# Pooled attention and a gated convolution FFN on one core: first k as words over SyncE, w_in whole over GpSimd, first expansion tiles split at 128 tokens, and a new written order

## The chip, the core and the metric

The kernel runs on one core of one Trainium2 chip. The core has TensorE (PE; its weight loads are shown apart as PEld), VectorE (DVE), ScalarE (ACT), GpSimd (POOL) and SyncE (SP), and 16 DMA engines, which loads and stores share. The metric is the device time of one execution in microseconds (us).

## What is computed

Eight batches, each of 8 heads, 576 tokens and 64 channels per head. k and v are averaged over groups of 8 tokens (72 groups), q attends to the averages, and the result, 576 x 512 per batch, goes through a gated FFN with a depthwise convolution of three taps along the tokens:

```python
k_p = k.reshape(B, H, Sp, pool, D).mean(axis=3)
v_p = v.reshape(B, H, Sp, pool, D).mean(axis=3)
attn = softmax(q @ k_p^T / sqrt(D))
x = attn @ v_p                          # heads side by side: (B, S, 512)
h = np.maximum(x @ w_in, 0.0)           # 512 -> 1024
conv_out[s] = sum(conv_w[t] * h[s + t - 1] for t in (0, 1, 2))
out = (h * sigmoid(conv_out)) @ w_out   # 1024 -> 512
```

Inputs and output are fp32; the kernel computes in bf16 with fp32 sums.

## The kernel before, in words

Everything is one list of small operations, each added to a `Planner` with its engine, what it reads and what it writes. Their order is not found at build time: `PARAMS["order"]` is a long string of operation numbers, written out, and the operations are issued in that order, so each engine runs its own share of the list strictly one after the other. An entry such as `17A1/159@B1` means: 17 fills (matmuls of zeros into PSUM buffer A1, line 227), then operation 159, whose result goes to PSUM buffer B1. There are five PSUM buffers, A0 to A2 (two banks) and B0, B1 (one bank); an operation that takes a buffer waits until the last reader of its former content is done. `PARAMS["act"]` lists the operations that could run on either engine and run on ACT; the others run on DVE. `PARAMS["alt"]` picks one of several ways for some steps.

Per batch b the steps are:

- Loads. k (`load_k`, lines 265 and 269), v (`load_v`, 277 and 282) and q (`load_q`, 246 and 251) go over POOL, which converts fp32 to bf16 on the way. Batches use the buffers `k_b`, `v_b`, `q_b` in turns of two. POOL's loads carry one of eight semaphores in turn, so each load waits until the one eight places ahead of it has landed.
- k: `pool8` adds eight tokens in steps on DVE (414, 418, 443, the sum `ksum`), PE transposes it (459), and two copies put it into `kz` (465). v: the same on DVE (414, 418, 491; for batch 0, 479 and 483), then two multiplications by a mask into `vblk` (503, 508). There is a second way, `by_identity`, in which PE adds the eight tokens by eight matmuls with the identity and one copy follows.
- q: PE transposes (525 for batch 0, 545 for others), copies bring it to `qT` (531, 552).
- Scores (583, 585; 602, 604), exponentials on ACT (591, 610), product with v on PE (628, 632), division by the sum on DVE (641 the reciprocal, 645 the multiplication into `xx`), transposition on PE (659) with a copy (663), or from batch 3 on by a transposing DMA on SP (668).
- Expansion `mm1` (685 for batch 0, 700 for others) with ReLU on ACT (691, 706). For batch 0 a block of 128 hidden units is done in two groups of tokens, 0 to 383 and 384 to 575, so that the first can start before the last tokens are there.
- Convolution, either by multiplications and additions (`conv_off`, 722 to 741) or on PE with diagonal matrices `dw` (`conv_pe`, 753; the matrices are made at 384 and 386), gate on ACT (741, 758), multiplications on DVE (785, 791).
- Output `mm2` (813), copy (836, 826), store on SP (840, 831) from one of three buffers `osb`.

At the start, the first two of four slices of the first half of w_in come as fp32 words over SP (line 290) and are converted by two copies (294); the other two come over POOL (301), the second half of w_in too (306).

## Time and profile before

| | |
|---|---|
| three runs | 198.35, 198.59, 198.66 us (median 198.59) |
| profiled execution | 199.99 us, span from first to last instruction 198.3 us |
| busy in the span | PE 190.1, DVE 164.1, ACT 172.0, POOL 48.3 us |
| granted TensorE clock, mean | 1.00 |
| read from device memory, written | 32.5 MB, 9.4 MB |

The page lists engines' busy time, the chain of work that ended last, and groups of instructions by line. The timeline lists instructions in order of time: start, length, engine, line, operation, result<-operands with shape and type, how many were merged, and in brackets how long the engine stood idle before and what ended that. Lengths of neighbours on one engine can overlap by 0.1 us or so, since they are pipelined.

### The profile page before, as it was taken

The page shows a single profiled execution, that of the slowest core. Times are in us where ns is not written, and L with a number is a line of the kernel's source. Part 1 is how long each engine was busy: PE and PEld are TensorE (multiplying, and loading weights), DVE is VectorE, ACT ScalarE, POOL GpSimd, SP SyncE. Part 2 cuts the span into 40 slices and gives each one's busy share as a digit, 9 for nine tenths or more (in the row PEclk, how much of TensorE's full clock was granted, in tenths as well). Part 3 has the DMA queues.
Part 4 walks back from the last instruction along what each step waited for, and adds up shares of the span by engine and source line. Part 5 has one row for each costly group of instructions (what it writes and reads, how often), then busy time and mean ns, then how long its engine had stood idle before and what let it go on. Part 6 is the DMA issues. An engine that isn't in the chain of part 4 may idle for free.

```text
span 198.3 us, 4826 instructions
## 1 busy us (share of the span) xinstructions
PE 190.1 (96%) x1890; PEld 132.3 (67%) x1905; DVE 164.1 (83%) x375; ACT 172.0 (87%) x314; POOL 48.3 (24%) x87
## 2 busy tenths in 40 slices
PE   7899989999999999999999999999999999999992
PEld 7897866776677878856866665766666655555441
DVE  3246759999949999999899999999999999899620
ACT  0559999992679999999999999999999899999931
POOL 7878425347225630080006100000000000000000
PEclk9999999999999999999999999999999999999999
DMA  6999999999999999999987999691401844043244
GB/s 134 169 135 150 188 205 205 206 191 142 204 196 185 152 192 60 197 113 197 172 232 158 194 213 166 120 164 26 172 3 27 266 144 161 1 148 117 106 164 159
DMA packets 40763, 30.41 MB, mean 153 GB/s; under 512 B 18572, under 2 KB 36004, under 8 KB 40740
## 3 DMA queue, kind: packets, MB, share of 16 engines
q0 software_dynamic: 18272, 16.00, 56.5%
q1 hardware_dynamic: 22468, 14.11, 31.4%
q8 instruction: 15, 0.25, 0.5%
q14 instruction: 8, 0.07, 0.1%
HBM read 32.52 MB, written 9.44 MB: 212 GB/s over the span
## 4 chain that ended last, share of the span: by engine, by line
PE 48%; ACT 16%; DMA 14%; DVE 12%; POOL 4%; issue 4%; ACTq 0%; DVEq 0%; POOLq 0%
PE psfA L700 16%; PE psfB L813 14%; DMA k_b<-in_k_dram 10%; ACT tg L741 5%; DMA v_b<-in_v_dram 4%; PE psfA L628 4%; ACT cv L722 3%; ACT hT L706 3%; PE psfA L753 2%; PE psfA L602 2%; ACT osb L836 2%; DVE cv L724 2%; POOL v_b L282 2%; DVE gT L791 2%; PE psfA L632 2%
## 5 line engine op out<-in xcount | busy, mean ns | idle before, releaser
L813 PE MATMUL psfB<-w_out,gT 128*128 128x512 bf16 (+1 forms) x259 | 62.6, 377 | 1.0 <-issue 0.2
L700 PE MATMUL psfA<-xT,w_in 128*128 128x288 bf16 x448 | 61.9, 286 | 0.1
L700 PEld LDWEIGHTS <-w_in 128*128 128x128 bf16 x448 | 43.0, 98 | 13.1 <-issue 0.8
L813 PEld LDWEIGHTS <-gT 128*128 128x128 bf16 x290 | 27.7, 98 | 28.8 <-DVE gT L791 1.0
L741 ACT ACTIVATE tg<-cv,cs 128x576 bf16<-128x576 bf16 x54 | 41.2, 789 | 0.3
L706 ACT ACTIVATE hT<-psfA 128x576 bf16<-128x576 f32 x56 | 36.6, 665 | 1.4 <-PE psfA L700 0.9
L645 DVE TENSOR_TENSOR xx<-psfA,rr 128x512 bf16<-128x512 f32 x40 | 27.1, 686 | 0.7
L722 ACT ACTIVATE cv<-hT,cr 128x576 bf16<-128x576 bf16 x35 | 26.9, 783 | 0.1
L724 DVE TENSOR_SCALAR cv<-hT,cr 128x576 bf16<-128x576 bf16 x73 | 25.9, 377 | 0.9 <-ACT hT L706 0.7
L282 POOL DMA_DIRECT2D v_b<-in_v_dram x32 | 16.8, 531 | 33.9 <-DVE vs L491 31.1
L836 ACT COPY osb<-psfB 128x512 f32<-128x512 f32 x33 | 19.2, 591 | 5.9 <-PE psfB L813 5.5
L791 DVE TENSOR_TENSOR gT<-tg,hT 128x1152 bf16<-128x1152 bf16 x32 | 23.9, 751 | 0.3
L610 ACT ACTIVATE attnT<-psfA 128x576 bf16<-128x576 f32 x35 | 22.7, 675 | 0.3
L734 DVE TENSOR_TENSOR cv<-cv 128x1152 bf16<-128x1152 bf16 (+1 forms) x29 | 20.7, 713 | 1.0 <-ACT cv L722 0.3
L729 DVE TENSOR_TENSOR cv<-cv,hT 128x1152 bf16<-128x1152 bf16 (+1 forms) x29 | 20.6, 711 | 0.3 <-ACT cv L722 0.2
L227 PEld LDWEIGHTS <-zero 128*128 128x128 bf16 x238 | 15.6, 105 | 1.7 <-DVE zero L318 1.1
L628 PE MATMUL psfA<-vblk,attnT 128*128 128x130 bf16 x160 | 15.9, 221 | 0.4 <-DVE xx L645 0.3
L785 DVE TENSOR_SCALAR tg<-tg 128x1152 bf16<-128x1152 bf16 x32 | 14.2, 448 | 2.2 <-ACT tg L741 2.0
L628 PEld LDWEIGHTS <-attnT 128*128 128x128 bf16 x160 | 11.8, 98 | 4.4 <-DVE xx L645 0.6
L227 PE MATMUL pswA<-zero 128*128 128x128 bf16 x192 | 13.3, 235 | 1.1 <-DVE zero L318 1.1
L414 DVE TENSOR_TENSOR k_b<-k_b 128x1280 bf16<-128x1280 bf16 x8 | 6.7, 840 | 6.8 <-DMA k_b<-in_k_dram 6.8
L641 DVE RECIPROCAL rr<-psfA 128x8 f32<-128x8 f32 x40 | 7.7, 198 | 5.2 <-PE psfA L632 5.1
(95 smaller groups left out, 234.1 us busy)
## 6 DMA issues: line engine op xcount, KB each, us to landing
out_dram<-osb SPq DMA_DIRECT2D x14, 512.0 KB, 3.2
k_b<-in_k_dram POOLq DMA_DIRECT2D x8, 512.0 KB, 8.5
q_b<-in_q_dram POOLq DMA_DIRECT2D x7, 576.0 KB, 8.2
v_b<-in_v_dram POOLq DMA_DIRECT2D x7, 512.0 KB, 12.2
out_dram<-osb SPq DMA_DIRECT2D x7, 256.0 KB, 2.1
w_out<-in_moe_w_out_dram POOLq DMA_DIRECT2D x2, 512.0 KB, 11.8
wf<-in_moe_w_in_dram SPq DMA_DIRECT2D x1, 512.0 KB, 5.3
k_b<-in_k_dram POOLq DMA_DIRECT2D x8, 64.0 KB, 6.3
```

The costliest lines, as they stand in the source:

```text
L227: nc.tensor.matmul(out=t, lhsT=zero[:, 0:P], rhs=zero[:, 0:P], start=True, stop=True)
L610: nc.scalar.activation(out=at(m)[:, t, :].rearrange("p (r i j) -> p r i j", i=2, j=3), in_=slot(key)[:, :, 0:HC].rearrange("p i (j r) -> p ...
L628: nc.tensor.matmul(out=a[:, g, c * w:(c + 2) * w], lhsT=attnT[m][:, S * s + u0:S * s + u0 + P], rhs=vblk[m][:, 2 * s:2 * s + 2, :].rearran ...
L645: nc.vector.tensor_tensor(out=xx[i3].rearrange("p (g h e) -> p g h e", g=2, h=4), in0=av_view()[:, :, :, 0:D], in1=rr[i3].rearrange("p (g ...
L700: nc.tensor.matmul(out=t[:, i, 0:HC], lhsT=w_in[:, c, f * P:(f + 1) * P], rhs=xT[m][:, c, i * HC:(i + 1) * HC], start=(c == 0), stop=(c == ...
L706: nc.scalar.activation(out=hT[m][:, f, 2:S + 2].rearrange("p (i x) -> p i x", i=2), in_=slot(key)[:, :, 0:HC], func=ACT.Relu)
L722: nc.scalar.activation(out=cv[y][:, kk // 2, z, :], in_=src, func=ACT.Copy, scale=sc)
L724: nc.vector.tensor_scalar(out=cv[y][:, kk // 2, z, :], in0=src, scalar1=sc, scalar2=None, op0=OP.mult)
L741: nc.scalar.activation(out=tg[i3][:, z, :], in_=cv[y][:, 0, z, :], func=ACT.Tanh if half else ACT.Sigmoid, scale=cs[:, f + z:f + z + 1] if ...
L791: nc.vector.tensor_tensor(out=o_, in0=tg[i3], in1=hT[b % 2][:, f:f + 2, 2:S + 2], op=OP.mult)
L813: nc.tensor.matmul(out=a[:, 0, j0:j1], lhsT=g[:, c, t * P:(t + 1) * P], rhs=w_out[:, c, j0:j1], start=(c == 0), stop=(c == n_fb - 1), skip ...
L836: copy_on(e)(out=osb[i3][:, x, :], in_=slot(key)[:, 0, :])
```

## The change

- k of batch 0 comes as fp32 words over SP (three loads, ahead of nearly everything) into the three output buffers `osb`, which are free until the first output. DVE's first addition reads the words there and writes bf16 into `k_b` (three instructions, one per buffer), and goes on as before.
- The first half of w_in comes whole over POOL with conversion; the words over SP and the two copies go.
- In the expansion of batch 0 the group of tokens 0 to 383 of the first four blocks of hidden units is split at 128 tokens, so that its first part needs only the first 128 tokens.
- v of batch 1 is summed on PE (`alt`: `"v1": 1`).
- `order` and `act` are written anew over the whole program; fills go from 238 to 167.

```diff
 "order": (
-    "59 0 45 58 2 40 49 46 39 50 41 57 56 48 13 1 16 3 57A0/4@B0 17 5 43 18 6 12A0/83@B0 36 53 7 20 52 84 55 61 69 38 23 54 28 14 73 25 "
+    "50 0 49 59 2 45 52 46 60 51 47 54 53 74 48 72 55 57 58 13 73 16 75 1 76 56 3 99A0/77@B0 39 14 78 15 79 20A0/80@B1 17 86 82@B0 40 "
...
-"alt": {"w": 1, "q1": 1, "c0.5": 2,
+"alt": {"q1": 1, "v1": 1, "c0.5": 2,
...
-    wf = st("wf", [P, n_dc, 512], FP32)
+    wf = st("wf", [P, 2, 512], FP32)
...
     def load_k(b):
-        m = b % 2
+        m = b % NK
         src = rows(k, b)
+        if b == 0:
+            for x in range(2):
+                def fn(e, x=x):
+                    nc.sync.dma_start(out=osb[x], in_=src[256 * x:256 * x + 256].rearrange("(t p) e -> p t e", p=P))
+                pl.add(f"ldkf{x}", "SP", 0.5, fn, writes=[("osb", x, 0), ("osb", x, 1)], dma=(256, 0.104, 16))
+
+            def fn(e):
+                nc.sync.dma_start(out=osb[2][0:64, 0, :], in_=src[512:576])
+            pl.add("ldkf2", "SP", 0.5, fn, writes=[("osb", 2, 0)], dma=(64, 0.104, 16))
+            return
...
+        def whole():
+            def fn(e):
+                nc.gpsimd.dma_start(out=w_in[:, :, 0:512], in_=src[:, :, 0:512])
+            pl.add("ldwi", "POOL", 0.8, fn, writes=[("wi", 0, c) for c in range(n_dc)], dma=(512, 0.087, 16))
...
         def on_dve():
-            pool8(b, "k", src, keys)
+            if b == 0:
+                for x, n in enumerate((2, 2, 1)):
+                    def fn(e, x=x, n=n):
+                        nc.vector.tensor_tensor(out=src[:, 2 * x:2 * x + n, 0:256], in0=osb[x][:, 0:n, 0:256], in1=osb[x][:, 0:n, 256:512], op=OP.add)
...
-                for c in range(n_dc):
-                    nc.tensor.matmul(out=t[:, 0, 0:n], lhsT=w_in[:, c, f * P:(f + 1) * P], rhs=xT[m][:, c, j0:j1],
+                wk = [("wi", f // 4, c) for c in range(n_dc)]
+                cut = P if x == 0 and f < 4 else 0
+                for a0, a1, ts_ in ((0, cut, ts[0:1]), (cut, n, ts[1 if cut else 0:])):
...
+                        for c in range(n_dc):
+                            nc.tensor.matmul(out=t[:, 0, a0:a1], lhsT=w_in[:, c, f * P:(f + 1) * P], rhs=xT[m][:, c, j0 + a0:j0 + a1],
```

In the pieces below a row is an instruction of one engine in its order: number, line, operation, result<-operands, shape, and the semaphores that it waits for; `_75` and `_76` are the two `v_b`, `_73` and `_74` the two `k_b`, `_77` and `_78` the two `q_b`.

POOL's first loads before, right behind the constants, and what stands ahead of q of batch 1 and w_in further on:

```order
6 L246 DMA q_b_77<-in_q_dram 32x8x384
7 L265 DMA k_b_73<-in_k_dram 128x4x512
8 L269 DMA k_b_73<-in_k_dram 64x512
9 L246 DMA q_b_77<-in_q_dram 64x8x384
10 L282 DMA v_b_75<-in_v_dram 16x512 [waits DVE_49]
...
29 L277 DMA v_b_75<-in_v_dram 128x2x512 [waits DMASW2_49]
30 L375 AFFINE_SELECT mask<-mask 128x4x65
31 L251 DMA q_b_78<-in_q_dram 96x8x384 [waits DMASW3_49]
32 L269 DMA k_b_74<-in_k_dram 64x512 [waits DMASW4_49]
33 L301 DMA w_in<-in_moe_w_in_dram 128x2x512 [waits DMASW5_49]
34 L265 DMA k_b_74<-in_k_dram 128x4x512 [waits DMASW6_49]
```

And now:

```order
6 L248 DMA q_b_77<-in_q_dram 64x8x384
7 L248 DMA q_b_77<-in_q_dram 32x8x384
8 L289 DMA v_b_75<-in_v_dram 128x2x512 x2
9 L294 DMA v_b_75<-in_v_dram 16x512 [waits DVE_49]
...
18 L389 AFFINE_SELECT mask<-mask 128x260
19 L253 DMA q_b_78<-in_q_dram 96x8x384 [waits DMASW0_49]
...
26 L302 DMA w_in<-in_moe_w_in_dram 128x4x512 [waits DMASW1_49]
27 L281 DMA k_b_74<-in_k_dram 64x512 [waits DMASW2_49]
28 L277 DMA k_b_74<-in_k_dram 128x4x512 [waits DMASW3_49]
```

k of batch 0 is gone from POOL, so q and v of batch 0 stand first, and q of batch 1, w_in and k of batch 1 stand behind loads that were issued at the very start.

The start of ACT before:

```order
1 L384 ACT_TABLE_LOAD [waits DVE_49]
2 L384 ACTIVATE dw_113<-ident,cw 128x128 [waits Pool_49]
3 L384 ACTIVATE dw_119<-ident,cw 128x128
4 L531 COPY qT_86<-psbB 128x24x32 [waits PE_49]
5 L294 COPY w_in<-wf 128x512 [waits DMAHW0_49]
```

The start of ACT now (L498 is the copy into `kz`, L564 that into `qT`, L624 the exponentials):

```order
1 L498 ACT_TABLE_LOAD [waits DVE_49]
2 L498 COPY kz_84<-psbB 64x4x72 [waits PE_49]
3 L498 COPY kz_84<-psbB 64x4x72
4 L564 COPY qT_86<-psbB 128x12x64 [waits PE_49] x2
5 L564 COPY qT_86<-psbA 128x24x32 [waits PE_49]
6 L624 ACTIVATE attnT_88<-psfB 128x384 [waits PE_49]
7 L624 ACTIVATE attnT_88<-psfA 128x384 [waits PE_49]
```

The `dw` matrices and the casts of w_in no longer come first; the table load stands with the copies of `kz`, and both halves of `kz` and all of `qT` are on ACT.

DVE between v of batch 4 and v of batch 6 now (L524 ends the sum of v, L434 and L438 are its first two additions):

```order
163 L524 TENSOR_TENSOR vs<-v_b_75 128x320
...
186 L772 TENSOR_TENSOR cv_102<-cv_102 128x1152
187 L434 TENSOR_TENSOR v_b_75<-v_b_75 128x5x256
...
191 L434 TENSOR_TENSOR v_b_76<-v_b_76 128x5x256
...
195 L438 TENSOR_TENSOR v_b_76<-v_b_76 128x5x128
...
213 L438 TENSOR_TENSOR v_b_75<-v_b_75 128x5x128
```

Before, with the lines of that kernel (L491, L414, L418):

```order
154 L491 TENSOR_TENSOR vs<-v_b_75 128x320
...
166 L414 TENSOR_TENSOR v_b_76<-v_b_76 128x5x256
...
178 L418 TENSOR_TENSOR v_b_76<-v_b_76 128x5x128
...
180 L414 TENSOR_TENSOR v_b_75<-v_b_75 128x5x256
```

v of batch 6 (`v_b_75`) is added ahead of v of batch 5 (`v_b_76`) instead of behind it, 24 rows behind the sum that frees its buffer instead of 26.

On PE the entry ahead of the transposes of k of batch 1 is `17A1/159@B1` where it had no fill, and the next expansion has 12 more.

81 lines of the change are left out of this document (49 added, 32 removed), and 93 rows, old and new, of the table PARAMS.

## The prediction

> **What bounds the kernel now.** I read the stretches first, then the order of time in the first 30 us, then the chain and the DMA issues. The stretches give busy time in the order PE, PEld, DVE, ACT, POOL, then the granted clock, the DMA share and GB/s.
>
> ```profile
> 0.00:24.00 24.00, 21.84 (x414) 19.84 (x414) 12.04 (x38) 14.30 (x36) 18.21 (x39) 1.00 0.98 154
> 30.00:45.00 15.00, 14.73 (x189) 10.98 (x187) 14.58 (x32) 14.39 (x30) 6.60 (x13) 1.00 1.23 199
> 45.00:190.00 145.00, 143.58 (x1223) 95.49 (x1235) 134.80 (x297) 134.77 (x229) 21.99 (x35) 1.00 0.84 146
> ```
>
> From 45 to 190 us PE is busy for 143.6 of 145.0 us, and DVE and ACT for 134.8 each: PE sets the pace there. From 30 to 45 us all three are full. In the first 24 us PE looks busy too, but most of that is fill (matmuls of zeros). So the time is the moment at which real PE work starts, plus the PE work behind it. What holds that start back is data:
>
> ```profile
> 2.08 8.71 DMA k_b<-in_k_dram
> 11.26 1.00 DVE L414 TENSOR_TENSOR k_b<-k_b 128x1280 bf16<-128x1280 bf16 x1 [3.62 <-DMA k_b<-in_k_dram]
> 13.25 0.49 DVE L443 TENSOR_TENSOR ksum<-k_b 128x640 bf16<-128x640 bf16 x1
> 14.32 0.45 PE L459 MATMUL psbA<-ident,ksum 128*128 128x128 bf16 x5
> 16.41 0.87 ACT L591 ACTIVATE attnT<-psfB 128x384 bf16<-128x384 f32 x2
> 19.05 0.40 PE L628 MATMUL psfA<-vblk,attnT 128*128 128x130 bf16 x4
> 23.99 0.82 PE L685 MATMUL psfB<-xT,w_in 128*128 128x384 bf16 x4
> ```
>
> The first row is of the chain that ended last, the others of the timeline (start, length). k of batch 0 is issued at 2.08 and lands at 10.79; DVE has waited 3.62 us for it; the sum over eight tokens is done at 13.74, the first exponential starts at 16.41, the first product with v at 19.05, the first expansion (L685) at 23.99. A second wait for data follows at k of batch 1:
>
> ```profile
> 16.03 11.00 DMA k_b<-in_k_dram
> 27.12 0.83 DVE L414 TENSOR_TENSOR k_b<-k_b 128x1280 bf16<-128x1280 bf16 x1 [3.17 <-DMA k_b<-in_k_dram]
> 28.30 0.49 PE L685 MATMUL psfA<-xT,w_in 128*128 128x192 bf16 x4
> 29.28 0.45 PE L459 MATMUL psbA<-ident,ksum 128*128 128x128 bf16 x5 [0.50 <-DVE ksum L443]
> ```
>
> **The change, step by step.** *k of batch 0.* It becomes 1.18 MB of words on SP's queue in place of a conversion on POOL's. The nearest rows are the words of w_in, which go, and the stretches in which they moved:
>
> ```profile
> 0.81 0.45 SPq L290 DMA_DIRECT2D wf<-in_moe_w_in_dram  x1
> wf<-in_moe_w_in_dram SPq DMA_DIRECT2D x1, 512.0 KB, 5.3
> 1.37 0.72 POOL L246 DMA_DIRECT2D q_b<-in_q_dram  x1 [0.86 <-POOLq L905]
> 3.00:4.00 1.00, 1.00 (x12) 1.00 (x11) 0.00 (x0) 0.00 (x0) 1.00 (x2) 1.00 0.88 302
> 4.00:5.00 1.00, 1.00 (x17) 1.00 (x15) 0.00 (x0) 0.00 (x0) 1.00 (x6) 1.00 1.30 220
> ```
>
> Issued at 0.81, 512 KB land 5.3 us later, at 6.1. Their bytes are through by about 4.8, so some 1.2 us of this is tail. The other 0.66 MB of k follow on the same queue: at the 302 GB/s of the fourth microsecond they take 2.2 us and land at 8.2; at half of the 220 GB/s of the fifth, which q then shares, 6.0 us and land at 12.0. I take 8.6, near the undisturbed end, because q, issued at 1.37, left the words nearly all of the fourth microsecond. The rule that speaks against this is in the Trainium skill (DMA: Bandwidth & Descriptors, Queues, rings and completion order): each DMA engine takes the queues that have work in turns, packet by packet. By that rule the half-share end is the likelier one and the sum would be that of the third rival below; the fifth microsecond, where the total fell to 220 GB/s with both queues at work, agrees as far as it goes.
>
> DVE then adds 128x512 elements from fp32 (L463, the last of three; the other two wait for earlier landings), halves again and sums. Prices from rows of the same size:
>
> ```profile
> 19.85 0.69 DVE L645 TENSOR_TENSOR xx<-psfA,rr 128x512 bf16<-128x512 f32 x1
> 12.78 0.44 DVE L418 TENSOR_TENSOR k_b<-k_b 128x640 bf16<-128x640 bf16 x1
> ```
>
> 8.6 + 0.69 + 0.44 + 0.49 = 10.2 for the sum, against 13.74: 3.5 us earlier.
>
> *ACT's first instruction.* Before, ACT loaded its function table while nothing waited. In the new order the load stands ahead of the copies of kz and waits with them for DVE's memset of kz (the order on ACT shows both), which is behind the sum and identf:
>
> ```profile
> 7.13 1.28 ACT L384 ACT_TABLE_LOAD   x1 [7.13 <-DVE cw L338]
> 6.16 0.38 DVE L330 CAST identf<-ident 24x24 f32<-24x24 bf16 x1 [3.55 <-POOL ident masks.py:199]
> 2.04 0.30 DVE L391 MEMSET kz<- 128x288 uint32 x1
> 15.57 0.39 ACT L465 COPY kz<-psbA 64x288 bf16<-64x288 bf16 x1
> 14.05 1.50 ACT L531 COPY qT<-psbB 128x768 bf16<-128x768 bf16 x2 [2.25 <-PE psbB L525]
> ```
>
> 10.2 + 0.38 + 0.30 = 10.9, + 1.28 = 12.2, two kz copies 0.78, three qT copies 3 x 0.75: the first exponential starts at 15.2, against 16.41. Of 3.5 us, 1.2 are left, since copies that stood beside other work are now in a row. The casts of w_in leave ACT (0.62 and 0.69 us); here nothing waits for them.
>
> *Exponentials to first expansion.* Before, 16.41 to 19.05 is 2.6 us. In the new order two scores reuse PSUM buffers that an exponential frees, and one more exponential and one dw stand ahead: about 3.1, so the first product with v starts at 18.3. From there the first expansion follows after five normalisations, whose last frees its PSUM buffer: two products (0.5 + 0.4), then five times 0.69, five reciprocals and a dw of 0.2 each, less some 0.5 of overlap: about 5.1 us, against 4.94. It starts at 23.4, **0.6 us earlier**. Splitting a 384-token group at 128 costs four weight loads more per block; by the L628 row above, four 130-column matmuls take 0.40 with their tail, so 0.1 each, 0.4 for four blocks. w_in, now whole over POOL, is no stop: its two neighbours ahead are out earlier, because POOL is no longer held by k.
>
> ```profile
> 13.98 0.80 POOL L251 DMA_DIRECT2D q_b<-in_q_dram  x1
> 15.31 0.75 POOL L301 DMA_DIRECT2D w_in<-in_moe_w_in_dram  x1
> 13.00:14.00 1.00, 0.76 (x36) 0.63 (x36) 0.71 (x2) 0.00 (x0) 0.99 (x3) 1.00 0.39 37
> ```
>
> Eight loads of 0.5 to 0.8 us and POOL's masks end at about 10, so q of batch 1 is issued near 10 where it was 13.98, w_in near 11.5 (15.31), k of batch 1 near 13 (16.03). The hole at 13 us (37 GB/s) closes, and k of batch 1 lands some 3 us earlier; the wait of 0.50 us ahead of L459 goes. If it doesn't, these 0.5 us stay.
>
> *Fill.* The four blocks end at 28.4 (28.79 before). But the new order puts 17 fills ahead of the transposes of k of batch 1; 23 took 1.33 us, so 17 take 1.0:
>
> ```profile
> 14.56 1.33 PEld L227 LDWEIGHTS <-zero 128*128 128x128 bf16 x23
> ```
>
> L459 starts at 29.4, 0.1 later than before. So the whole gain of the start is spent here, unless these fills stand in a wait anyway.
>
> *From there to the first output product.* The rows of before:
>
> ```profile
> 39.51 0.81 DVE L414 TENSOR_TENSOR v_b<-v_b 128x1280 bf16<-128x1280 bf16 x1
> 40.36 0.49 DVE L418 TENSOR_TENSOR v_b<-v_b 128x640 bf16<-128x640 bf16 x1
> 40.89 0.33 DVE L491 TENSOR_TENSOR vs<-v_b 128x320 bf16<-128x320 bf16 x1
> 41.03 1.17 PE L227 MATMUL pswB<-zero 128*128 128x128 bf16 x18
> 38.73 1.82 PE L753 MATMUL psfA<-hT,dw 128*128 128x288 bf16 x12
> 45.17 1.89 PE L813 MATMUL psfB<-w_out,gT 128*128 128x512 bf16 x7
> ```
>
> L459 to L813 takes 15.9 us, with 33 fills (1.9 us, by the entries of the order table): PE is ahead of DVE there and pads. v of batch 1 leaves DVE (0.81 + 0.49 + 0.33 = 1.6 us) for eight matmuls of 320 columns on PE; by the L753 row (12 of 288 in 1.82 with the tail, 0.14 each) they cost 1.1, and ACT gets one copy for it. ACT has some 3 us less to do behind this point (dw tiles and q copies moved to DVE, which was idle while it waited for k). PE's list up to the first L813 comes to 13.5 us up to the first product with v of batch 1 and 2.1 behind it, 15.6 in all with 29 fills, and is 0.7 us of work further on when it gets there. So this stretch gives 0.3 + 0.7 = 1.0, less 0.2 for a stall or two: bounds 0 (DVE and ACT still bind) and 1.6 (all of DVE's relief counts). I take **0.8**.
>
> *Behind it* PE has the same matmuls in another sequence; only copies and multiplications change sides between ACT and DVE, both about 9 us below PE from 45 to 190 us. I count nothing.
>
> **Sum:** +0.1 - 0.8 = -0.7 us. On the span that is 198.3 to 197.6, on the profiled execution's 199.99 it is 199.3. The median of the runs, 198.59, lies 1.4 below the profiled execution; the same difference gives **197.9**.
>
> **Rivals.** *First, a larger gain.* The words land at 8.2 and the 17 fills stand where PE would have waited: 0.4 and 1.0 more, 196.5. For it: PE waited 0.50 at that place before. Against it: k of batch 1 should now be early.
>
> *Second, the gain is swallowed.* The stretch up to L813 gives its lower bound 0, since DVE and ACT were full there too (14.58 and 14.39 of 15): 198.6.
>
> *Third, slower: the words lose the race with q.* q's loads go out first on POOL, at 1.37, and if the two queues share evenly the words land at 12.0, 3.4 us after my value; each microsecond goes straight through to the first expansion. From a landing at about 9.3 on there is no gain; at 12.0 the time is 197.9 + 3.4 = 201.3. PE's clock adds to it: its 99 fills end at 8.2 (57 took 4.79 us; of 58 ns each they would take 3.3, so 26 or so ran at half speed, some 3 us, and 42 more take 2.4), and L459 would come at 13.7.
>
> ```profile
> 1.05 4.79 PEld L227 LDWEIGHTS <-zero 128*128 128x128 bf16 x57 [1.05 <-DVE zero L318]
> ```
>
> A gap of 5.5 us is longer than the start-up that ran slow, and the transposes and scores behind it (about 2 us of PE on the chain) could run at half speed again, 1 to 2 us more. The Trainium skill (TensorE: Matmul & The Clock Gate, Part 1: The HAM clock gate) puts this fall at one idle window of about 3.4 us; by that rule my forecast's gap, 8.2 to 10.3, leaves the clock alone, and no gap in the trace of before is long enough to test it.
>
> *Fourth, slower in the middle.* The new order adds v of batch 6 ahead of v of batch 5 on DVE:
>
> ```profile
> 84.54 0.27 DVE L491 TENSOR_TENSOR vs<-v_b 128x320 bf16<-128x320 bf16 x1
> 88.71 0.78 POOL L277 DMA_DIRECT2D v_b<-in_v_dram  x1
> 96.96 0.83 DVE L414 TENSOR_TENSOR v_b<-v_b 128x1280 bf16<-128x1280 bf16 x1 [0.68 <-DMA v_b<-in_v_dram]
> ```
>
> The buffer is free at 84.8; its load lands just ahead of 96.96, and DVE already waited 0.68 us. The new order leaves DVE about 2.2 us less work between the two, while POOL issues the load 2.5 us sooner and has three small ones behind it. If it lands where it did, DVE waits 2.9 us, 2.2 more, and where that reaches PE the time is 200.1. It decides once it exceeds the 0.7 gained. Against it: PE has 1.9 us more to do before it needs v of batch 5.
>
> **How the numbers follow.** Forecast 0.42, larger gain 0.15, swallowed 0.12, third 0.13, fourth 0.18. About 0.2% (0.4 us) is what a measurement of this kernel can tell from no change. Of the forecast 0.06 falls inside that, with the swallowed case: same 0.18; faster 0.36 + 0.15 = 0.51; slower 0.31. The range goes from 195.9 (larger gain with the upper bound 1.6 of the second stretch) to 200.3; above lies most of the third rival, below little.
>
> **What would show it.** The last L463 starts at 8.6 (7 to 9.3 right, 11 or more wrong); ACT_TABLE_LOAD starts near 10.9 and the first exponential near 15.2; the first expansion near 23.4; L459 of batch 1 near 29.4 without a wait ahead of it; the first L813 near 45.0. A wait of DVE over 1.5 us for v of batch 6, or a clock below 1.00 after 10 us, would make it wrong.

## The result, and the profile after

The changed kernel takes 207.55 us (median of 4 runs, 206.39 to 208.61) against 198.62 us (198.35 to 198.73) for the kernel before: a ratio of 1.045, with a 95% interval of 1.0393 to 1.0507. The forecast was 197.9 us; the third rival had the sign and two of the causes, the shared DMA engines and PE's clock, but at 201.3 us and one or two more it was priced far too low. Each ratio below is against runs of the kernel before in the same batch, whose medians go from 199.2 to 199.6 us. Ratios and medians leave out five executions, one of e1, one of h1 and three of g2, that were over 1.5% slower than the fastest of their kernel (the traces of h1 and g2 are of two of them).

The stretches of the changed kernel, in the columns of before (PE, PEld, DVE, ACT, POOL, granted clock, DMA share, GB/s):

```profile
0.00:24.00 24.00, 16.08 (x240) 13.79 (x241) 8.83 (x24) 7.44 (x15) 14.53 (x34) 0.73 0.90 163
30.00:45.00 15.00, 14.76 (x206) 12.24 (x204) 11.62 (x37) 14.91 (x38) 3.32 (x6) 1.00 1.19 195
45.00:190.00 145.00, 142.80 (x1258) 97.25 (x1271) 137.50 (x308) 132.47 (x227) 26.35 (x42) 1.00 0.76 140
```

The two later rows hardly differ from before. The first does: ACT is busy for 7.4 us in place of 14.3, and the mean granted clock of TensorE is 0.73. The page's row of slices (5.14 us each; a digit is the clock in tenths of full speed, and 9 means 90% or more) and two stretches say when:

```profile
PEclk9955579999999999999999999999999999999999
```

```profile
8.00:11.00 3.00, 0.23 (x5) 0.06 (x1) 1.07 (x4) 0.00 (x0) 2.22 (x4) 1.00 1.18 232
11.00:28.00 17.00, 12.49 (x171) 10.10 (x172) 8.52 (x23) 8.98 (x20) 11.05 (x26) 0.50 0.98 152
```

PE stands idle behind its 99 fills, and from 11 to 28 us it runs at half clock, although it is busy for 12.5 of those 17 us. The timeline gives the order of events:

```profile
7.79 0.43 DVE L463 TENSOR_TENSOR k_b<-osb 128x256 bf16<-128x256 f32 x1 [5.34 <-DMA osb<-in_k_dram]
8.78 1.49 POOL L294 DMA_DIRECT2D v_b<-in_v_dram  x3 [4.61 <-DVE v_b L429]
10.96 0.69 DVE L463 TENSOR_TENSOR k_b<-osb 128x512 bf16<-128x512 f32 x1 [1.93 <-DMA osb<-in_k_dram]
12.31 0.49 DVE L473 TENSOR_TENSOR ksum<-k_b 128x640 bf16<-128x640 bf16 x1
12.72 1.42 DVE L344 CAST identf<-ident 24x24 f32<-24x24 bf16 x1
12.86 0.71 PE L492 MATMUL psbB<-ident,ksum 128*128 128x128 bf16 x5 [4.63 <-DVE ksum L473]
14.05 0.80 POOL L253 DMA_DIRECT2D q_b<-in_q_dram  x1
14.50 1.28 ACT L498 ACT_TABLE_LOAD   x1 [14.50 <-DVE vblk L409]
16.65 0.85 PE L558 MATMUL psbB<-ident,q_b 64*64 64x64 bf16 x24 [0.16 <-ACT kz L498]
17.43 1.46 PE L558 MATMUL psbA<-ident,q_b 32*64 32x32 bf16 x48
19.62 0.50 ACT L624 ACTIVATE attnT<-psfB 128x384 bf16<-128x384 f32 x1
23.82 0.59 PE L661 MATMUL psfA<-vblk,attnT 128*128 128x130 bf16 x4 [2.07 <-ACT attnT L624]
30.20 0.39 PE L723 MATMUL psfA<-xT,w_in 128*128 128x128 bf16 x4
35.76 0.44 PE L492 MATMUL psbB<-ident,ksum 128*128 128x128 bf16 x5
52.26 1.89 PE L851 MATMUL psfB<-w_out,gT 128*128 128x512 bf16 x7
```

The last words are there at 10.94, not at 8.6 (issued at 2.44 and landed 8.5 us later); the sum of k is done at 12.80, still 0.9 us ahead of before. Then everything stands in a row: the transposes of k (L492), 20 fills, the table load, the copies of kz, and only behind them the last two of the three groups of q transposes (L558), at half clock. The first exponential is 3.2 us later than before, the first expansion 6.2, the first output product 7.1, and so is the end (span 205.5 against 198.3). The work behind the first output product is what it was: 153.2 us against 153.1.

The loss at the first output product, stretch by stretch (differences of the times above and of those quoted of before):

| stretch | before | after | loss |
|---|---|---|---|
| to the sum of k | 13.74 | 12.80 | -0.94 |
| sum of k to first exponential | 2.67 | 6.82 | 4.15 |
| first exponential to first expansion | 7.58 | 10.58 | 3.00 |
| to the transposes of k of batch 1 | 5.29 | 5.56 | 0.27 |
| to the first output product | 15.89 | 16.50 | 0.61 |

### The profile page after: what moved, and what is told of

Same layout as the page of the kernel before. It is cut to its first block, busy times and chain, and to the rows that moved or that the text cites. A ratio compares the mean times of both kernels' runs of the same rounds, so it can differ in the third digit from the quotient of the medians.

```text
span 205.5 us, 4736 instructions
## 1 busy us (share of the span) xinstructions
PE 191.1 (93%) x1843; PEld 133.6 (65%) x1858; DVE 167.6 (82%) x387; ACT 166.4 (81%) x301; POOL 46.7 (23%) x85
## 4 chain that ended last, share of the span: by engine, by line
PE 56%; DVE 11%; issue 10%; DMA 9%; ACT 7%; POOL 4%; SPq 1%; ACTq 0%; DVEq 0%; POOLq 0%
PE psfB L851 23%; PE psfA L738 17%; DMA osb<-in_k_dram 4%; DMA v_b<-in_v_dram 3%; PE psfA L661 3%; PE psfA L851 2%; DMA qT<-q 2%; PE psfA L635 2%; DVE gT L829 2%; PE psfA L665 2%; PE psfB L723 1%; DVE xx L678 1%; POOL v_b L289 1%; POOL v_b L294 1%; ACT hT L729 1%
## 5 line engine op out<-in xcount | busy, mean ns | idle before, releaser
L851 PE MATMUL psfB<-w_out,gT 128*128 128x512 bf16 (+1 forms) x259 | 61.3, 377 | 0.8
L738 PE MATMUL psfA<-xT,w_in 128*128 128x288 bf16 x448 | 60.9, 286 | 0.7 <-DVE xx L678 0.7
L738 PEld LDWEIGHTS <-w_in 128*128 128x128 bf16 x448 | 42.9, 98 | 13.6 <-DVE xx L678 1.0
L744 ACT ACTIVATE hT<-psfA 128x576 bf16<-128x576 f32 x56 | 37.4, 683 | 2.1 <-PE psfA L738 1.8
L678 DVE TENSOR_TENSOR xx<-psfA,rr 128x512 bf16<-128x512 f32 x40 | 27.1, 684 | 0.6
L760 ACT ACTIVATE cv<-hT,cr 128x576 bf16<-128x576 bf16 x35 | 27.4, 827 | 0.1
L294 POOL DMA_DIRECT2D v_b<-in_v_dram x32 | 16.9, 535 | 43.2 <-DVE vs L524 22.2
L762 DVE TENSOR_SCALAR cv<-hT,cr 128x576 bf16<-128x576 bf16 x73 | 25.0, 369 | 1.9 <-ACT hT L729 1.8
L874 ACT COPY osb<-psfB 128x512 f32<-128x512 f32 x33 | 20.0, 617 | 6.6 <-PE psfB L851 5.5
L661 PE MATMUL psfA<-vblk,attnT 128*128 128x130 bf16 x160 | 16.6, 230 | 2.4 <-ACT attnT L624 2.1
L661 PEld LDWEIGHTS <-attnT 128*128 128x128 bf16 x160 | 12.5, 103 | 6.2 <-issue 2.2
L823 DVE TENSOR_SCALAR tg<-tg 128x1152 bf16<-128x1152 bf16 x32 | 14.7, 469 | 2.0 <-ACT tg L779 1.7
L229 PEld LDWEIGHTS <-zero 128*128 128x128 bf16 x167 | 12.5, 114 | 1.8 <-DVE zero L332 1.1
L229 PE MATMUL pswA<-zero 128*128 128x128 bf16 x153 | 12.2, 251 | 1.1 <-DVE zero L332 1.1
L498 ACT ACT_TABLE_LOAD x1 | 1.3, 1283 | 14.5 <-DVE vblk L409 14.5
## 6 DMA issues: line engine op xcount, KB each, us to landing
w_in<-in_moe_w_in_dram POOLq DMA_DIRECT2D x2, 512.0 KB, 10.2
```

Of the source, the lines that this page charges most:

```text
L229: nc.tensor.matmul(out=t, lhsT=zero[:, 0:P], rhs=zero[:, 0:P], start=True, stop=True)
L661: nc.tensor.matmul(out=a[:, g, c * w:(c + 2) * w], lhsT=attnT[m][:, S * s + u0:S * s + u0 + P], rhs=vblk[m][:, 2 * s:2 * s + 2, :].rearran ...
L678: nc.vector.tensor_tensor(out=xx[i3].rearrange("p (g h e) -> p g h e", g=2, h=4), in0=av_view()[:, :, :, 0:D], in1=rr[i3].rearrange("p (g ...
L738: nc.tensor.matmul(out=t[:, i, 0:HC], lhsT=w_in[:, c, f * P:(f + 1) * P], rhs=xT[m][:, c, i * HC:(i + 1) * HC], start=(c == 0), stop=(c == ...
L744: nc.scalar.activation(out=hT[m][:, f, 2:S + 2].rearrange("p (i x) -> p i x", i=2), in_=slot(key)[:, :, 0:HC], func=ACT.Relu)
L760: nc.scalar.activation(out=cv[y][:, kk // 2, z, :], in_=src, func=ACT.Copy, scale=sc)
```

## The experiments

Theories at the start: the **clock** (PE idle, then half speed), **POOL** held by a memset that stands behind the first addition of words on DVE, the **table load** in the chain, and the **sharing** of the DMA engines by words, q and v. The numbers in the order table: 48 is that memset, 74, 72, 73 are the additions of words, 59 and 60 the loads of q, 53 to 58 those of v, 13 to 17 and 1 masks and identity, 77 the transposes of k, 80, 82, 84 those of q, 81, 83 copies of q, 114 the first product with v.

### One cause at a time

**e1** adds fills at one place.

```diff
-99A0/77@B0
+178A0/77@B0
```

> The changed kernel with one number altered: 178 fills instead of 99 ahead of the transposes of k of batch 0 (79 more of 58 ns, 4.6 us, the length of PE's idle time from 8.23 to 12.86). Clock theory: the granted clock fell at 11.0 because PE stood idle, and the half speed from 11.0 to 28.07 costs about 3 of the 6.2 us by which the first expansion (L723) is late; now the clock stays full, the three groups of q transposes take half as long, the first exponential starts near 18.1 (19.62 in the changed kernel), the first expansion near 27 (30.20), and the time is about 204.5. Waiting theory: the start waits for DVE, POOL and the loads in any case, PE's speed is not in the chain; then the first expansion stays within 0.5 us of 30.2 and the time near 207.5.

Median 205.95 us, ratio 1.035 (1.0277 to 1.0424), an interval that overlaps the changed kernel's. The first exponential starts at 18.49 and the first expansion at 28.22, 2.0 us earlier than in the changed kernel. The clock is part of the loss, but less than I expected. Not all of the 2.0 us need be the clock either: the cast `identf`, which stands ahead of the table load, took 0.17 us in this execution and 1.42 in that of the changed kernel. And the clock fell all the same, later:

```profile
22.03 0.39 PE L661 MATMUL psfA<-vblk,attnT 128*128 128x130 bf16 x4 [2.07 <-ACT attnT L624]
20.30:23.70 3.40, 1.38 (x20) 1.25 (x20) 1.27 (x5) 1.93 (x8) 1.24 (x2) 1.00 1.21 197
23.80:27.10 3.30, 3.17 (x44) 2.98 (x46) 3.08 (x9) 2.17 (x7) 1.29 (x2) 0.50 1.23 201
```

Here it fell behind 3.4 us in which PE was busy for 1.38, with a wait of 2.07 us for the exponentials among them, and it came back 3.4 us later.

**e2** moves the memset.

```diff
-"50 0 49 59 2 45 52 46 60 51 47 54 53 74 48 72
+"50 0 49 48 59 2 45 52 46 60 51 47 54 53 74 72
```

> The changed kernel with one memset (a v_b tail) moved on DVE from behind the first addition of words to ahead of it, so that POOL no longer waits 4.61 us for it. POOL theory: the masks and the identity are ready near 8, the conversion identf takes 0.4 instead of 1.42, the table load on ACT starts near 13.5 (14.50), q of batch 1 is issued near 10.6 (14.05), the first expansion comes 1 us or more earlier (29.2 or less), the time is about 206.3. Clock theory: PE still waits from 8.2 to 12.8 for the sum of k, the clock still falls at 11 and most of the loss stays, 206.5 to 207.5. If the loads now go out earlier and slow the words of k, the last addition of words starts later than 10.96 and the time is above 207.5.

Median 206.14 us, ratio 1.0357 (1.0307 to 1.0406). POOL is freed as expected (q of batch 1 at 10.78, identf 0.16 us, the table load at 13.05), the first exponential comes 0.6 us earlier, and of that 0.1 us is left at the first expansion (30.11): PE was at half clock until 28.65. So the hold on POOL is real, and in this trace it costs next to nothing at the start. The four runs leave room for more: their median is 1.4 us below the changed kernel's, but the intervals overlap, and executions of equal mean clock (0.975) differ by 0.5 to 0.7 us (spans 203.6 and 203.8 against 204.3). Where that would come from was not traced.

**e3** loads the table early.

```diff
-            nc.vector.memset(zero, 0.0)
+            nc.vector.memset(zero, 0.0); nc.scalar.copy(out=cs[:, 0:1], in_=zero[:, 0:1])
```

> The changed kernel with one copy of one column on ACT at the very start, so that ACT loads its function table there and not ahead of the copies into kz. Table theory: the copies into kz start near 14.5 (15.80), the second group of q transposes near 15.4 (16.65), the first exponential near 18.3 (19.62), the first expansion near 28.9 (30.20), time about 206.3. Rival: PE at half clock is the limit there (three groups of transposes of 0.85, 0.85 and 1.46 us from 15.64 on), the table load lies beside it, and less than 0.4 us is gained.

Median 206.57 us, ratio 1.0382 (1.033 to 1.0434). In the profiled execution the words landed 1.1 us later (the last addition at 12.11), so the first exponential stayed at 19.63; from the sum of k to it the time fell from 6.82 to 5.67, a part of it because the clock was full from 16.9 to 20.3 there and the cast `identf` took 0.17 us. So the table load is worth 1.15 us at most; at the first expansion (29.58) 0.6 us are left.

**e4** gives the words the DMA engines first.

```diff
-"50 0 49 59 2 45 52 46 60 51 47 54 53 74 48 72 55 57 58 13 73 16 75 1 76 56 3 99A0/77@B0
+"50 0 49 48 2 45 52 46 51 47 13 16 1 14 15 17 41 44 59 60 54 53 55 57 58 56 74 72 73 75 76 3 99A0/77@B0
```

> The changed kernel with the memset of the tail of v_b early as in e2 and POOL's constants (masks, identity, paddings) ahead of the loads of q and v of batch 0, so that the words of k have the DMA engines to themselves for about 4 us. Sharing theory: the words are late (10.96) because q and v move beside them; alone, 1.18 MB land near 6, the last addition of words starts near 6 and the sum is done near 8; PE has no gap, the clock stays full, and although q and v now land 2 to 4 us later, the first expansion comes near 25 and the time is about 202. Queue theory: the words go at their own pace whatever else moves; then the last addition of words still starts near 11, the clock falls, q and v are later on top, and the time is above 208.

Median 202.35 us, ratio 1.0154 (1.0108 to 1.0199): two thirds of the loss are gone with loads moved, not one added or removed. Timeline, and two stretches:

```profile
6.52 1.70 DVE L463 TENSOR_TENSOR k_b<-osb 128x256 bf16<-128x256 f32 x3 [3.78 <-DMA osb<-in_k_dram]
15.06 0.50 ACT L624 ACTIVATE attnT<-psfB 128x384 bf16<-128x384 f32 x1
26.18 0.39 PE L723 MATMUL psfA<-xT,w_in 128*128 128x128 bf16 x4
11.30:14.70 3.40, 1.96 (x81) 1.63 (x76) 0.17 (x1) 2.34 (x5) 1.53 (x3) 1.00 1.21 188
14.80:24.90 10.10, 7.60 (x73) 5.62 (x73) 6.50 (x20) 5.85 (x17) 5.40 (x10) 0.50 1.23 195
```

The last words are there at 7.50 in place of 10.94: the sharing theory holds. The difference is larger than that between executions: with q and v issued beside the words, the last addition starts between 10.85 and 12.76 in seven traces (the changed kernel, e1, e2, e3, e7, e9a, e9b), and with them behind the words near 7.5 in two (e4, e5). The expectation of a full clock does not hold; it fell at 14.7, after 3.4 us in which PE was busy for 1.96.

### Is it the words, or the order?

**h1** has the order, fills and choices of the kernel before, and only the loads changed.

```diff
 def load_k(b):
...
+        if b == 0:
+            for x in range(2):
+                def fn(e, x=x):
+                    nc.sync.dma_start(out=osb[x], in_=src[256 * x:256 * x + 256].rearrange("(t p) e -> p t e", p=P))
...
-"alt": {"w": 1, "q1": 1, "c0.5": 2,
+"alt": {"q1": 1, "c0.5": 2,
```

> The kernel before with its own order, fills and choices, but k of batch 0 as words over SP into the output buffers (and w_in whole over POOL, since its words would stand behind k's on SP). Order theory: the words are not what costs, the written order around them is; here the table load and the dw matrices still come first on ACT, POOL is not held, PE has its fills, so the clock stays full; the words land near 10.8 as the converted k did (10.79), the sum of k is done 0 to 1 us earlier than 13.74, and the time is 197.8 to 199.2. Words theory: fp32 words beside q and v are themselves what makes the start late; the last addition of words starts at 11.5 or later, the first expansion after 24.5, and the time is above 200.

Median 198.75 us, ratio 0.9954 (0.9923 to 0.9985): a little **faster** than the kernel before. The words are not what costs, and the order theory holds. The last words landed at 10.13 there and the sum of k was done at 12.12, but 81 fills kept PE until 13.75:

```profile
9.05 4.70 PE L230 MATMUL pswA<-zero 128*128 128x128 bf16 x81
```

**h2** has only v of batch 1 on PE.

```diff
-"alt": {"w": 1, "q1": 1, "c0.5": 2,
+"alt": {"w": 1, "q1": 1, "v1": 1, "c0.5": 2,
...
-160 257 246 162 300 247 18B0/305@A1
+256@A2 245 299 246 158@B0 159 161 304@A1
```

> The kernel before with one choice altered: v of batch 1 is summed by eight matmuls with the identity on PE and one copy on ACT, in the place of 18 fills; DVE loses three instructions (0.81 + 0.49 + 0.33 = 1.6 us). Theory of the prediction's second stretch: DVE binds before the first output product, which comes 0.3 to 1.0 us earlier than 45.17; time 197.6 to 198.9. Rival: the matmuls and the copy on ACT (1.25 and 0.43 us in the changed kernel) stand on the path that DVE leaves, the first output product comes no earlier than 45.0 and the time is 198.9 to 200.

Median 200.24 us, ratio 1.0019 (0.9985 to 1.0053), which cannot be told from no change. The stretch that I had counted on, of the timeline of h2:

```profile
29.39 0.45 PE L459 MATMUL psbA<-ident,ksum 128*128 128x128 bf16 x5 [0.95 <-DVE ksum L443]
41.15 1.25 PE L429 MATMUL psfB<-v_b,ident 128*128 128x320 bf16 x8
45.77 1.89 PE L813 MATMUL psfB<-w_out,gT 128*128 128x512 bf16 x8
```

It takes 16.38 us, 0.5 more than the 15.89 before. The eight matmuls take as long (1.25) as the 18 fills that they replace (1.17), so PE gains nothing; that DVE's relief is not what PE waits for there is argued, not shown. In all kernels that keep the changed kernel's order behind the start this stretch takes 16.50 to 16.52 us (e6 and e8, which do not, take 17.7).

### How much is the clock, how much the order

**e5** is e4 with fills in PE's waits (8 more than the expectation counts, ahead of a transpose of x).

```diff
-99A0/77@B0 ... 82@B0 ... 84@A0 ... 114@A0 ... 122@B1
+116A0/77@B0 ... 8A0/82@B0 ... 16A0/84@A0 ... 26B1/114@A0 ... 8B1/122@B1
```

> The kernel of e4 (words alone at first, POOL's constants ahead of q and v) with 17, 8, 16 and 26 fills more where PE waited at 8.4, 11.4, 12.4 and 17.1, so that the clock does not fall at 14.73. Clock theory: with a full clock to the end the scores and products with v take half the time, the first exponential starts near 14.8 (15.06 in e4), the first product with v near 18.5 (19.11) and the first expansion near 24.3 (26.18); time about 200.3 (202.35 in e4). Rival: the exponentials on ACT and the normalisations on DVE set this stretch; the first expansion stays at 25.7 or later and the time at 202.

Median 201.79 us, ratio 1.0136 (1.0087 to 1.0185), not to be told from e4. The clock stays full, as the stretch of e4's half clock shows, and from the first exponential to the first expansion it takes 9.05 us in place of 11.12:

```profile
14.80:24.90 10.10, 8.82 (x180) 7.27 (x174) 7.00 (x23) 6.96 (x19) 5.14 (x8) 1.00 1.24 200
16.13 0.50 ACT L624 ACTIVATE attnT<-psfB 128x384 bf16<-128x384 f32 x1
25.18 0.39 PE L723 MATMUL psfA<-xT,w_in 128*128 128x128 bf16 x4
```

But q landed 1 us later in this execution (its first transposes start at 11.80, where it was 10.82), and the 16 fills ahead of its third group (1.07 us) then came on top: half of the gain was lost ahead of the first exponential.

**e6** and **e8** are written starts of my own that were to mend everything at once.

```diff
-3 99A0/77@B0 39 78 79 20A0/80@B1
+39 13 16 1 3 14 15 17 40 41 44 59 60 54 53 55 57 58 56 70A0/4@B1 5 6 7 8 10 9 11 12 22 26 74 72 73 75 76 40A0/77@B0
```

> The changed kernel with a new written start: words alone and POOL's constants ahead of q and v (as e4), the function table loaded at the very start (as e3), memsets, identity and weights of the convolution ahead of the words on DVE, all ten scores of batch 0 ahead of the products with v, q of batch 1 transposed behind the first expansions, and fills in PE's waits. If the four causes named so far (POOL held, table load in the chain, words beside q and v, clock at half) are all there is, the first exponential starts near 13.5, v is summed near 18, the first product with v starts near 18.2, the first expansion near 23.2 (23.99 before), and the time is 197.0 to 198.5, at or below the kernel before. If the first expansion comes after 24.5 something else holds the start: v of batch 0, which lands near 16 in e4, is the one I would look at.

Median 208.24 us, ratio 1.0425 (1.0376 to 1.0473), 10 us above the expectation: a miss, and a useful one.

```profile
7.27 2.41 PE L229 MATMUL pswA<-zero 128*128 128x128 bf16 x40
8.96 1.62 DVE L463 TENSOR_TENSOR k_b<-osb 128x256 bf16<-128x256 f32 x3
11.69 0.45 PE L492 MATMUL psbB<-ident,ksum 128*128 128x128 bf16 x5 [2.01 <-DVE ksum L473]
12.30:25.80 13.50, 11.94 (x165) 9.39 (x163) 2.67 (x8) 6.22 (x15) 7.32 (x12) 0.50 1.18 183
22.06 2.77 PE L229 MATMUL pswA<-zero 128*128 128x128 bf16 x24
```

The words were there before 8, but DVE was still busy with weights that waited behind 70 fills. PE then stood idle for 2.0 us, the clock fell, and 24 fills that were to keep it up took 2.77 us at half speed, ahead of the first product with v. Fills that are placed by a time that does not come cost twice: they hold up the work behind them, and the wait that they were to fill stays.

```diff
-70A0/4@B1 5 6 7 8 10 9 11 12 22 26 74 72 73 75 76 40A0/77@B0
+46A0/4@B1 5 6 74 72 73 75 76 64A0/77@B0 78 79 7 8 10 9 11 12 22 26
```

> The written start of e6 with the two faults that its trace shows mended: the weights of the convolution are made behind the sum of k and not ahead of it (there they let the first addition of words wait until 8.96), and the fills ahead of the transposes of k are 64 after 46 in place of 40 after 70, so that PE does not stand idle for the 2.0 us before 11.69 in which the clock fell; one copy of q goes to DVE. Theory: the sum of k is done near 9.3, the clock stays full, the first exponential starts near 13.5, v binds then and the first product with v starts near 18, the first expansion near 23 (28.63 in e6, 25.18 in e5); time 197.5 to 199. Rival: the order of the scores and of q of batch 1 was not what cost 1.5 us between the first exponential and the first expansion in e5; then the first expansion comes after 24.5 and the time is above 200.

Median 203.06 us, ratio 1.0177 (1.0113 to 1.0241), 4 us above the expectation. The first exponential comes at 13.02 and the first expansion at 23.91, as in the kernel before, in spite of a clock that fell at 14.5 once more. But the transposes of k of batch 1 start at 31.91, 8.0 us behind it (5.56 in the changed kernel, 8.0 in e6 too): the order that I had written behind the first expansion loses this time. Which entry of it does was not traced.

**e7** keeps the loads where the change has them and makes three repairs.

```diff
-99A0/77@B0 ... 82@B0 ... 114@A0
+172A0/77@B0 ... 8A0/82@B0 ... 26B1/114@A0
```

> The changed kernel with three repairs that leave its loads where they are: the memset of the tail of v_b ahead of the words on DVE (as e2), the function table loaded at the very start (as e3), and 73, 8 and 26 fills more ahead of the transposes of k, of the second group of q, and of the first product with v, so that the clock stays full. If these three causes add up, the sum of k is done near 12.7, the first exponential starts near 16.9 (19.62 in the changed kernel), and with a full clock 9.05 us later (as from 16.13 to 25.18 in e5) the first expansion near 26 (30.20); time about 202.5. What is then left against the kernel before (2 us at the first expansion, 0.5 us before the first output product) belongs to the written order itself. If the first exponential stays later than 18, one of the three was not a cause.

Median 204.80 us, ratio 1.0267 (1.0205 to 1.0329). The same 17 us as above, with the clock full:

```profile
11.00:28.00 17.00, 14.81 (x311) 12.59 (x309) 10.28 (x36) 11.40 (x27) 8.85 (x19) 1.00 1.20 187
14.52 0.56 PE L558 MATMUL psbB<-ident,q_b 64*64 64x64 bf16 x24
15.57 0.56 PE L558 MATMUL psbB<-ident,q_b 64*64 64x64 bf16 x24
17.73 0.50 ACT L624 ACTIVATE attnT<-psfB 128x384 bf16<-128x384 f32 x1
26.28 0.38 PE L723 MATMUL psfA<-xT,w_in 128*128 128x128 bf16 x4
48.35 1.89 PE L851 MATMUL psfB<-w_out,gT 128*128 128x512 bf16 x7
```

From the sum of k (12.97) to the first exponential it takes 4.76 us (6.82 in the changed kernel), from there to the first expansion 8.55 (10.58): 4.1 us repaired. The expectation for the first expansion was right; 17.73 was 0.8 late: the 20 fills of the changed kernel and 8 of mine stand between the transposes of k (13.03) and the two groups of q (14.52 and 15.57). The time was 2 us above the expectation; some of it lies behind the first output product and was not traced.

**e9a** moves two groups of q transposes ahead of those of k.

```diff
-172A0/77@B0 39 14 78 15 79 20A0/80@B1 17 86 8A0/82@B0 40 81 84@A0 41 83
+139A0/80@B1 81 82@A1 83 22A0/77@B0 39 14 78 15 79 17 86 40 84@A0 41
```

> The kernel of e7 with the two large groups of q transposes and their copies put ahead of the transposes of k on PE and ACT (as in the kernel before; q of batch 0 lands near 10.5, the sum of k is done near 13.0), with 139 and 22 fills ahead of them in place of 172 and 20. Theory: in e7 the copies of kz, the transposes of q and their copies stand in a row behind the sum of k; now only kz and the third group follow it, the first exponential starts near 16.0 (17.73 in e7), the first expansion near 24.6 (26.28), the time falls by about 1.5 us against e7. Rival: the loads of q set this (second load landing near 12), and less than 0.5 us is gained.

Median 201.05 us, ratio 1.0069 (1.0042 to 1.0097). This one move takes 2.6 us off:

```profile
10.91 0.56 PE L558 MATMUL psbB<-ident,q_b 64*64 64x64 bf16 x24 [0.24 <-DMA q_b<-in_q_dram]
11.31 0.54 PE L558 MATMUL psbA<-ident,q_b 64*64 64x64 bf16 x24
13.11 0.45 PE L492 MATMUL psbB<-ident,ksum 128*128 128x128 bf16 x5
15.15 0.50 ACT L624 ACTIVATE attnT<-psfB 128x384 bf16<-128x384 f32 x1
23.70 0.38 PE L723 MATMUL psfA<-xT,w_in 128*128 128x128 bf16 x4
45.75 1.89 PE L851 MATMUL psfB<-w_out,gT 128*128 128x512 bf16 x7
```

The q transposes, and the 28 fills that stood ahead of them (1.6 us at 58 ns), now lie in the wait for the words. The first expansion is 0.3 us ahead of the kernel before, the first output product 0.6 behind it, which is the 0.6 us of the stretch with v of batch 1 (0.3 gained, 0.3 and 0.6 lost in the two stretches behind). So of the 4.5% that the changed kernel loses, the three repairs of e7 take off 1.8 points and this move 2.0, and 0.7 are left.

**e9b** changes the order around the first product with v as well.

```diff
-26B1/114@A0 119@A1 124@A2
+14B1/114@A1 119@A2 124@A0
...
-18 156@B1 25 130 30 118 131 154@A2 157 158 152@B0 135
+18 25 130 30 118 131 158 135
...
+24 199 156@B1 157 154@A2 155 152@B0 66
```

> The kernel of e9a, and besides: the first product with v goes to the PSUM buffer that the fifth exponential frees in place of the eighth, one dw leaves ACT's row ahead of it, and the three groups of transposes of q of batch 1 with two of their copies stand behind the first expansion's first block and not between the products with v and the transposes of x. Theory: from the first exponential to the first expansion it takes 7.6 us as in the kernel before (8.55 in e7), so the first expansion comes near 23.6 and the time falls by another 1 us. Rival: the chain of normalisations on DVE sets that stretch and it stays at 8.4 or more; or q of batch 1 is now late for the block behind, the transposes of k of batch 1 start as late as in e9a, and nothing is gained.

Median 203.19 us, ratio 1.0165 (1.0104 to 1.0227). From the first exponential (16.61, the words were 1.5 us later in this execution) to the first expansion (24.47) it takes 7.86 us in place of 8.55. All of that 0.7 lies ahead of the first product with v, which starts 2.84 us behind the first exponential in place of 3.55; the run changes the PSUM buffer, the dw and the fills (12 fewer) there together, so which of them it is stays open. Behind it nothing moves (5.02 us against 5.00), so taking q of batch 1 out of there gained nothing; PE waits for the normalisations instead (0.94, 0.43 and 0.31 us for `xx`). And q of batch 1 is now late: from the first expansion to the transposes of k of batch 1 it takes 7.35 us in place of 5.55. The second rival holds, and the time is 2 us above e9a's.

### A version that beats both

**g1** is h1 with fewer fills.

```diff
-81A0/80@B0
+46A0/80@B0
```

> The kernel of h1 (order of before, k as words, w_in whole over POOL) with 46 instead of 81 fills ahead of the first large group of q transposes. In h1 the sum of k was done at 12.12 and q of batch 0 had landed at 11.22, but 81 fills kept PE until 13.75. Theory: these fills hold the gain back; with 46 they end near 11.7, the transposes of k start near 12.7 (14.55 in h1), the first exponential near 14.8 (16.65), the first expansion 1 to 2 us earlier than 24.23, and the time is 196.8 to 198.0. Rival: v of batch 0 (landed 14.20, summed behind kz on DVE) or w_in and k of batch 1 come next, the first expansion or the transposes of k of batch 1 move by less than 0.5 us, and the time stays at h1's 198.7.

Median 197.98 us (196.96 to 198.48) against 199.27, ratio **0.9913** (0.988 to 0.9945).

```profile
9.32 2.74 PE L230 MATMUL pswA<-zero 128*128 128x128 bf16 x46
12.88 0.45 PE L493 MATMUL psbA<-ident,ksum 128*128 128x128 bf16 x5
14.98 0.87 ACT L625 ACTIVATE attnT<-psfB 128x384 bf16<-128x384 f32 x2
43.25 1.89 PE L852 MATMUL psfB<-w_out,gT 128*128 128x512 bf16 x7
```

The sum of k is done at 12.30 and PE takes it at 12.88; the first output product comes 1.9 us ahead of before, and the profiled span is 195.7 us.

**g2** adds the two remaining parts of the change to g1.

```diff
-                cut = 0
+                cut = P if x == 0 and f < 4 else 0
...
-"alt": {"q1": 1, "c0.5": 2,
+"alt": {"q1": 1, "v1": 1, "c0.5": 2,
```

> The kernel of g1 (order of before with 46 fills in place of 81, k as words, w_in whole over POOL) with the two other parts of the change as well: the first expansion tiles split at 128 tokens (each first piece directly ahead of its second, so that only the price of the split shows) and v of batch 1 summed on PE in the place of 18 fills. It has every part of the change but the written order. Theory: the parts are cheap and the order is what costs; the split costs some 0.4 us and v of batch 1 on PE some 0.5 between the transposes of k of batch 1 and the first output product (15.89 to 16.38 us in h2), so the time is 198.3 to 199.3, within 0.5% of the kernel before. Rival: the parts are dear by themselves; the time is above 201.

Median 198.71 us, ratio 0.9946 (0.9908 to 0.9983). Every part of the change is in this kernel except its written order, and it is faster than the kernel before, by 0.5%. The two parts cost g1 about 0.3%, which the intervals do not tell from nothing; in the traces, the stretch with v of batch 1 takes 16.55 us against g1's 16.06, the same 0.5 as in h2.

## Why the prediction was wrong, point by point

By the forecast's sum the first output product is at 44.5 us (45.17 less 0.7; the 45.0 given as a sign of being right does not follow from that sum). It came at 52.26. Of these 7.8 us, 2.6 lie up to the sum of k, 1.8 from there to the first exponential, 2.4 from there to the first expansion and 1.4 in the stretch to the first output product; the transposes of k of batch 1 give 0.4 back. So three steps failed ahead of the first expansion: the words were taken near their undisturbed price, the q transposes were not seen in PE's row, and the clock was put at nothing. A fourth is behind it, the gain from v of batch 1. One by one:

- **Where the words land** (8.6 taken, bounds 8.2 and 12.0): 10.94. The working asked who shares in the fourth microsecond and took the end near the undisturbed price. But the last of q's loads and v's large ones starts to be issued at 3.44 us, and e4, with them behind, has the words at 7.50. The Trainium skill (DMA: Bandwidth & Descriptors, Queues, rings and completion order) had the engines take their queues in turns; by that rule the half-share end was the likelier one, and the runs agree with it (10.94 beside q and v, 7.50 alone). This was 2.3 us of the forecast, and with it alone the forecast's own rule (no gain from 9.3 on) gives a slower kernel. Against before it is no loss: the sum of k was still 0.9 us earlier.
- **From the sum to the first exponential** (10.2 to 15.2, so 5.0): 6.82. This is the step that turned the earlier sum into a loss. It added ACT's instructions, "two kz copies 0.78, three qT copies 3 x 0.75", and left out that on PE the q transposes stand behind those of k, which wait for the sum, and that they take their PSUM buffers from the copies. The kernel before did them while it waited. e9a measures this place alone, with its 28 fills, at 2.66 us (4.76 to 2.10 from the sum to the first exponential); 8 of the fills, 0.5 us, are e7's own, so 2.2 are the changed kernel's at full clock. The table load, which was in the sum, is worth 1.15 there at most.
- **PE's clock** (nothing in the forecast; "1 to 2 us more" in the third rival): half for 17 us. Between e7 and the changed kernel, with the clock, the table and POOL together, lie 2.06 us ahead of the first exponential and 2.03 behind it; behind it the two differ in the clock and in the fills that hold it, so the clock has 2.0 there, and e4 and e5 give the same (11.12 to 9.05). The forecast's gap, 8.2 to 10.3, looked safe. It was not sure to be: e6 lost the clock behind a gap of 2.0 us, while e9b kept it through one of 1.96. The Trainium skill (TensorE: Matmul & The Clock Gate, Part 1: The HAM clock gate) puts the fall behind an idle window of about 3.4 us that runs freely; a window of that length agrees with the runs, a wholly idle one does not: the clock fell after 3.4 us with PE busy for 1.96 (e4), 1.38 (e1) or, of 3.3 us, 1.29 (e6).

```profile
8.80:12.10 3.30, 1.29 (x24) 1.11 (x22) 2.77 (x8) 0.00 (x0) 0.30 (x2) 1.00 1.25 197
```

- **First exponential to first expansion** (3.1 + 5.1 = 8.2): 10.58, of which 2.0 is the clock. With the clock full the changed order takes 8.55, so this term was only 0.35 too small: 3.55 for 3.1 up to the first product with v and 5.00 for 5.1 behind it.
- **Loads of batch 1 some 3 us earlier** (q near 10): q was issued at 14.05 and k of batch 1 at 16.49, later than before, because POOL waited 4.61 us for a memset that stands on DVE behind the first addition of words. The order rows of POOL showed the wait for DVE, and I didn't ask what stands ahead of that memset. In e2's trace it is worth 0.1 us at the first expansion.
- **Fills and the split**: 5.56 us to the transposes of k of batch 1, where the forecast had 6.0 (23.4 to 29.4; its own terms, 4.8 for the blocks, 0.4 for the split and 1.0 for the fills, give 6.2). Right in kind, and 0.4 too dear.
- **The stretch to the first output product** (0.8 us gained, bounds 0 to 1.6): 0.61 lost. The sign was wrong, outside the bounds; h2 shows v of batch 1 on PE doing 0.5 of it alone, and g2 against g1 the same.
- **Behind it** nothing: 153.2 against 153.1 us. Right. The fourth rival did not come: DVE waited 1.05 us for v, against 0.68 before.
- **The third rival** had the landing between its bounds and both its parts, sharing and clock. It took 5.5 us of gap for 1 to 2 us of slow PE; the slow clock went on for 17 us. No rival had the q transposes behind those of k.

With the clock full, the changed order still takes 1.0 us more between the first exponential and the first expansion than before (8.55 against 7.58). Nearly all of it lies ahead of the first product with v (3.55 against 2.64 us), and e9b gives back 0.7 there. What stays open: the remaining 0.2 us, why the clock stayed at half for five times 3.4 us (see the last section), and the differences of up to 1 us behind the first output product from one execution to another.

## What to carry to other kernels

When a change brings data earlier, follow PE's own row too: everything that could be done while it waits must stand ahead of the instruction that waits. Count a late instruction's followers on every engine, and price a wait of PE by the stretch that then runs at half clock, not by the wait itself. Fills belong to the time at which the data come: when that time moved by 1.6 us, 35 fills taken out brought the first output product from 44.92 to 43.25 us (h1 to g1; of the two ratios the intervals overlap), and an order written for other times cost 5% (1.045 against 0.9946 for g2, which has all the same parts).

## What the runs showed of the hardware

- The half-clock stretches have lengths in steps of 3.4 us. By the granted clock in the traces they go from 11.05 to 28.05 in the changed kernel (17.0 us), 23.7 to 27.1 in e1 (3.4), 13.5 to 16.9 and 20.3 to 27.1 in e3 (3.4 and 6.8), 14.7 to 24.9 in e4 (10.2), 12.2 to 25.8 in e6 (13.6) and 14.4 to 21.2 in e8 (6.8). The mean clocks of single executions differ by such steps too: 0.975 of the changed kernel's 204.3 us is 10.2 us at half speed, 0.958 of its 205.5 is 17.3. That this depends on where an execution's waits fall is argued, not shown.
- PE's busy time in the profile does not tell which way the clock goes. It fell behind 3.4 us with PE busy for 1.38 (e1), 1.96 (e4) and 2.74 (e8), but e9b kept it, although wherever one lays a row of stretches of 3.41 us over its trace, one of them has PE busy for 2.04 or less. Once fallen, it stayed at half through 3.4 us in which PE was busy throughout (the changed kernel, first line), and came back behind 3.4 us with 2.71 busy (e3, second line):

```profile
17.90:21.30 3.40, 3.40 (x55) 1.97 (x51) 2.08 (x8) 2.23 (x5) 2.50 (x5) 0.50 1.27 204
13.50:16.90 3.40, 2.71 (x25) 2.66 (x25) 1.12 (x4) 0.79 (x2) 3.33 (x15) 0.50 0.09 11
```

  What differs is what PE did: small q transposes and scores in the first, mostly fills of 128x128 in the second. No run here takes the two apart, so a forecast of the clock from busy time alone is a guess.
- One DVE cast of 24x24 elements took 1.42 us in the changed kernel while POOL worked on the masks, and 0.16 in e2, where POOL had finished them. It was 0.17 in e1 and e3, where POOL issued a load meanwhile. It was seen in one kernel only and not tested further.
